# A fused attention and gated-MLP kernel: a PSUM bank, a normalisation, and the order of the first batch

## The chip, the cores and the metric

The kernel runs on one core of a Trainium2 chip. The metric is the device time of one execution in microseconds; the lower the better. The core has five engines that run their own instruction streams in order and meet through semaphores: PE (matrix multiply), DVE (vector), ACT (scalar and activation functions), POOL (GpSimd) and SP, which here only issues DMAs. PE writes to PSUM, which is used here as eight banks.

## The reference

Grouped-query attention over 8 batches, then a gated MLP whose gate mixes along the sequence. Cut to what matters:

```python
# q (8, 16, 384, 64); k, v (8, 4, 384, 64); each k, v head serves 4 q heads
attn = softmax(q @ k.T / sqrt(64))          # rows sum to 1
x = (attn @ v), heads side by side          # (8, 384, 1024)
h = maximum(x @ w_in, 0)                    # w_in (1024, 1024)
u, v = h[..., :512], h[..., 512:]
v_n = (v - mean(v)) / sqrt(var(v) + 1e-6)   # over the 512 columns
v_s = einsum('ts,bsd->btd', w_spatial, v_n) + b_spatial[None, :, None]
out = (u * v_s) @ w_out                     # w_out (512, 1024), out float32
```

## The kernel before

**Two streams on PE.** Attention is written as steps. A batch has NU = 18 of them: six groups m (three query tiles qt times two head blocks j), each with three key tiles t. `scores(n)` (L224) makes one step's scores: two matmuls `sc` of a 64-row contraction (L233), one for each half of the rows, and one exponential on ACT that writes `aT` (L240). Two score tiles exist (pool ps_sc, bufs=2). `weigh(b, m, hh)` (L242) multiplies a group's three `aT` tiles with v: 12 matmuls `av` (L247) into the one bank of pool ps_av; then DVE takes the reciprocal `r` of the row sums (L257) and writes the normalised `x` (L259). `x_transposes` (L271) turns x into `xt` with PE (four transposes `xps`, a DVE copy, L276); later batches use DMA transposes (`x_turn`, L278) instead. `q_transposes` (L195) and `k_transposes` (L185) do the same for q and k of batches 0 and 1, their copies on DVE (L205, L193).

The MLP is a generator, `stream()` (L467), which hands out one matmul at a time and says how many columns it took. `v_tile(b, st)` (L288) makes one tile of 128 tokens of v: eight matmuls `pv` (L294), one for each 128 of the contraction; the first four read the blocks of xt that group m = 2 st gives, the last four those of m = 2 st + 1. After the eighth, DVE takes `vr` (maximum with 0, L304), `stats` and the aggregate `mv` (L306, L307). `normal(b)` (L311) makes v_n: ACT computes `rstd` by Ln and Exp (L314, L315), DVE `nmr` = -mean * rstd (L316), then POOL computes vr * rstd + nmr for the tiles `vn` (L327; in the last batch, tile 1 on DVE and tile 2 on ACT, L324). `u_tile` and `u_block` make u, `gate` the spatial product `psp` (L378) and the gating, `project` the output.

**The order.** It is written out by hand, and no scheduler changes it. The loop at L637 takes the steps n one after another; in each: DMAs and casts due at this step (`todo`), scores, the two halves of `weigh` (group m's first half at step 18b + 3m + 3, its second one step later), the `turns` due at this step (transposes, idle matmuls), and then `run_fill(cols)` (L631), which draws matmuls from the stream until the credit of columns is used up. HV = 8 x 512 columns is the work of one v tile. Up to step 17, scores are issued one step ahead, one a step; from step 18 two at each even step. In the first batch the fill gets a quarter of HV at steps 10 to 13 and two fifths at 16 to 20. Batch 0's x transposes of group m stand at step 3m + 6, for m = 5 at 20; its q transposes of (j, t) at 3(2t + j) - 3; k and q transposes of batch 1 at 14 to 16, 19 and later.

**Banks.** Pool ps_ck has three banks under one tag, "ck". Every transposed tile, pv, pu, psp and po takes one in turn, and gives it back when its last reader is done. The tile `warm` (L543) takes one for the idle matmuls of `keep_warm` (L545), which multiply the identity with itself and whose result nobody reads; as one tile serves all calls, its bank is held from the first call to the last, at step 15. The calls are of 27, 4 and 6 matmuls before the first scores, and then of 4 each at steps 0 to 9, 14 and 15.

**Loads.** w_in comes as four DMAs from POOL (L121): the v columns of contraction blocks 0 to 3, then of 4 to 7, then the u columns in the same two halves. POOL also casts k, q and v to fp16 ahead of each batch.

Of the kernel before, what the change touches and what calls it, by code (L numbers as in the profile page):

```python
# [9 lines left out]
FP32 = mybir.dt.float32  # L10
FP16 = mybir.dt.float16
AF = mybir.ActivationFunctionType
ALU = mybir.AluOpType
# [4 lines left out]
def kernel(  # L18
# [16 lines left out]
    nc = tc.nc  # L35
    P = 128
    B, HQ, S, D = q.shape
# [4 lines left out]
    NT = S // P  # L42
# [4 lines left out]
    scale = D ** -0.5  # L47
    VW = D + 2
    NU = 18
# [7 lines left out]
    small = ctx.enter_context(tc.tile_pool(name="small", bufs=4))  # L57
# [3 lines left out]
    ps_ck = ctx.enter_context(tc.tile_pool(name="ps_ck", bufs=3, space=PSUM))  # L61
# [29 lines left out]
    def load_q0(j, lo, hi, eng):  # L91
# [18 lines left out]
            name=nc.get_next_instruction_name(), act_func_set_id=set_id, ins=[], outs=[]  # L110
# [113 lines left out]
    def scores(n):  # L224
        b, r = divmod(n, NU)
        m, t = divmod(r, NT)
        qt, j = divmod(m, 2)
        if t == 0:
            aTs[b, m] = att.tile([P, NT, 2, 512], FP16, name=f"aT_{b}_{m}", tag="aT", bufs=3)
        sc = ps_sc.tile([P, 2, 512], FP32, name=f"sc_{b}_{m}_{t}", tag="sc")  # L230
        for hh in range(2):
            half = slice(hh * D, (hh + 1) * D)
            nc.tensor.matmul(  # L233
                sc[:, hh],
                kTs[b][half, j, t * P : (t + 1) * P],
                qTs[b, j][half, qt],
                start=True,
                stop=True,
            )
        nc.scalar.activation(aTs[b, m][:, t], sc, AF.Exp, scale=scale)  # L240

    def weigh(b, m, hh):  # L242
        qt, j = divmod(m, 2)
        av = ps_av.tile([P, G, D + 1], FP32, name=f"av_{b}_{m}_{hh}", tag="av")
        for i in range(G):
            for t in range(NT):
                nc.tensor.matmul(  # L247
                    av[:, i, :],
                    aTs[b, m][:, t, hh, i * P : (i + 1) * P],
                    v1[b % 2][:, 2 * j + hh, t, 0 : D + 1],  # L250
                    start=(t == 0),
                    stop=(t == NT - 1),
                )
        if m == 0 and hh == 0:
            x16s[b] = att.tile([P, NT, NB, P], FP16, name=f"x16_{b}", tag="x16")
        r = small.tile([P, G, 1], FP32, name=f"r_{b}_{m}_{hh}", tag="r")
        nc.vector.reciprocal(r, av[:, :, D : D + 1])  # L257
        blk = 4 * j + 2 * hh
        nc.vector.tensor_tensor(  # L259
            x16s[b][:, qt, blk : blk + 2].rearrange("p k (i d) -> p (k i) d", i=2),  # L260
            av[:, :, 0:D],
            r.to_broadcast([P, G, D]),
            ALU.mult,
        )
# [21 lines left out]
    mvs, v_rs, v_ns, uTs, gTs, osbs = {}, {}, {}, {}, {}, {}  # L286
# [22 lines left out]
        yield 512  # L309

    def normal(b):  # L311
        rstd = small.tile([P, NT], FP32, name=f"rstd_{b}", tag="rstd")
        nmr = small.tile([P, NT], FP32, name=f"nmr_{b}", tag="nmr")
        nc.scalar.activation(rstd, mvs[b][:, :, 1], AF.Ln, bias=eps_t)  # L314
        nc.scalar.activation(rstd, rstd, AF.Exp, scale=-0.5)  # L315
        nc.vector.scalar_tensor_tensor(  # L316
            nmr, mvs[b][:, :, 0], -1.0, rstd, op0=ALU.mult, op1=ALU.mult
        )
        v_ns[b] = []
        for st in range(NT):  # L320
            vn = moe.tile([P, DH], FP16, name=f"vn_{b}_{st}", tag="vn", bufs=6)
            a, c = rstd[:, st : st + 1], nmr[:, st : st + 1]
            if b == B - 1 and st == 2:
                nc.scalar.activation(vn, v_rs[b][st], AF.Identity, scale=a, bias=c)  # L324
            else:
                by = nc.vector if b == B - 1 and st == 1 else nc.gpsimd
                by.tensor_scalar(vn, v_rs[b][st], a, c, op0=ALU.mult, op1=ALU.add)  # L327
            v_ns[b].append(vn)

    def uT_tile(b):  # L330
# [4 lines left out]
    def u_tile(b, st):  # L335

        pu = ps_ck.tile([P, NM, P], FP32, name=f"pu_{b}_{st}", tag="ck")
        for m in range(NM):
            for kt in range(NB):
                if st == 1 and m == 1 and kt == 0:  # L340
                    normal(b)
                nc.tensor.matmul(  # L342
                    pu[:, m],
                    w_in16[:, kt, m * P : (m + 1) * P],
                    x_tile(b)[:, st, kt],
                    start=(kt == 0),
                    stop=(kt == NB - 1),
                )
                if m < NM - 1 or kt < NB - 1:
                    yield P  # L350
        nc.vector.tensor_scalar(
            uT_tile(b)[:, :, st * P : (st + 1) * P], pu, 0.0, None, op0=ALU.max
        )
        yield P

    def u_block(b, m):
        pu = ps_ck.tile([P, 512], FP32, name=f"pu_{b}_{m}", tag="ck")
        for kt in range(NB):
            nc.tensor.matmul(  # L359
                pu[:, 0:S].rearrange("p (t s) -> p t s", t=NT),  # L360
                w_in16[:, kt, m * P : (m + 1) * P],
                x_tile(b)[:, :, kt],
                start=(kt == 0),
                stop=(kt == NB - 1),
            )
            if m == 0 and kt == 3:
                normal(b)
            if kt < NB - 1:
                yield S
        nc.scalar.activation(uT_tile(b)[:, m, :], pu[:, 0:S], AF.Relu)  # L370
        yield S
# [123 lines left out]
    HV = NB * 512  # L495
# [41 lines left out]
    def turn_at(n, f, *args):  # L537

        turns.setdefault(n, []).append((f, args))

    by_dve, by_act = nc.vector.tensor_copy, nc.scalar.copy

    warm = ps_ck.tile([P, 512], FP32, name="warm", tag="ck")  # L543

    def keep_warm(n):  # L545
        for _ in range(n):
            nc.tensor.matmul(warm[:, 0:P], ident16, ident16, start=True, stop=True)  # L547

    keep_warm(27)
    cast_k(0, dve, (0,))  # L550
    cast_q(0, 0, dve, 0, 1, by_act)
    k_transposes(0, 0, by_dve)
    keep_warm(4)
    q_transposes(0, 0, 0, by_act, by_dve)
    keep_warm(6)
    scores(0)
    cast_k(0, pool, (1,))
# [18 lines left out]
    for j in range(2):  # L576
        for t in (1, 2):
            turn_at(3 * (2 * t + j) - 3, q_transposes, 0, j, t, by_dve)
    for n in (*range(10), 14, 15):
        turn_at(n, keep_warm, 4)  # L580
    at(9, cast_k, 1, pool)
    at(10, cast_q, 1, 0, pool)
# [46 lines left out]
    total = NU * B  # L629

    def run_fill(cols):  # L631
        nonlocal owed
        owed += cols
        while owed > 0:
            owed -= next(fill, 1e9)

    for n in range(total + 6):  # L637
        for f, args in todo.pop(n, []):
            f(*args)
        if n + 1 < NU:  # L640
            scores(n + 1)
        elif n >= NU and n % 2 == 0 and n < total:
            scores(n)
            scores(n + 1)
        for hh in range(2):
            b, r = divmod(n - 3 - hh, NU)
            if n >= 3 + hh and r % 3 == 0 and b < B:
                weigh(b, r // 3, hh)
        for f, args in turns.pop(n, []):
            f(*args)  # L650
        if n < NU + 3:

            run_fill(HV / 4 if 10 <= n < 14 else 2 * HV / 5 if 16 <= n else 0)
        elif n < 2 * NU + 4:
            run_fill((4 * HV + NM * NT * S + 6 * NM * 512) / (NU + 4 - 3))
        else:
            run_fill(COLS / NU)
# [31 lines left out]
```

## Time and profile before

| | us |
|---|---|
| median of 3 runs | 251.71 (251.39 to 252.03) |
| profiled execution | 251.51 |
| its span, first to last instruction | 249.7 |
| ACT busy | 169.1 |
| DVE busy | 139.9 |
| POOL busy | 97.4 |

The span is what the trace covers; the rest of the profiled execution's time lies around it. The timeline gives for each merged group of instructions its start, its length, engine, line, operation, tiles (out<-in), shapes and count, and in brackets the idle time of the engine before it with what ended it. A group's length on PE holds the drain of its last matmul, so consecutive PE groups overlap; the start of the next group tells when PE went on. PEld is PE's weight load, which runs beside its matmuls.

Landings of the first DMAs that the steps below need, by the trace: w_in's v columns at 13.50 and 16.86 us, its u columns at 25.42 and 27.86; k of batch 1 at 18.07, its q halves at 20.48 and 22.84, its v at 29.06.

### The profile page before, as it was taken

What the parts mean: (1) busy time and instruction counts of PE and PEld (TensorE: products, weight loads), DVE (VectorE), ACT (ScalarE), POOL (GpSimd) and SP (SyncE); (2) the same over time, 40 slices, a digit from 0 to 9 for tenths busy, and PEclk for the clock granted to TensorE, in tenths of its full rate; (3) what the DMA queues carried; (4) which work ended last, traced back from release to release, by engine and by line L of the source; (5) the groups of instructions that cost most, each with busy time, mean ns of one, the idle gap of its engine ahead of it and who ended that gap; (6) DMA issues with size and microseconds to landing.
All of it is one profiled execution on the core that took longest, in us unless ns stands there. A gap on an engine that the chain in (4) does not pass through costs nothing.

```text
span 249.7 us, 6038 instructions
## 1 busy us (share of the span) xinstructions
PE 240.9 (96%) x2438; PEld 126.2 (51%) x2438; DVE 139.9 (56%) x370; ACT 169.1 (68%) x217; POOL 97.4 (39%) x141
## 2 busy tenths in 40 slices
PE   7998998999999999999999999999999999999993
PEld 7564666634455445544455445544455444554551
DVE  2455777764546646375536746375536746375662
ACT  3896665777686677868686677868686687862231
POOL 2698836881034800393034800393034000350130
PEclk9999999999999999999999999999999999999999
DMA  7999998999379973996479973999474172024206
GB/s 180 269 285 252 301 281 238 289 233 265 104 145 326 173 276 66 236 274 178 168 145 333 169 273 71 206 302 175 171 151 90 24 273 45 0 46 168 84 26 230
DMA packets 73980, 46.93 MB, mean 188 GB/s; under 512 B 48112, under 2 KB 68912, under 8 KB 73952
## 3 DMA queue, kind: packets, MB, share of 16 engines
q1 hardware_dynamic: 68832, 37.63, 59.2%
q0 software_dynamic: 4080, 8.65, 13.9%
q8 instruction: 19, 0.31, 0.5%
q10 hardware_dynamic: 1040, 0.26, 0.5%
q14 instruction: 9, 0.07, 0.1%
HBM read 25.95 MB, written 12.58 MB: 154 GB/s over the span
## 4 chain that ended last, share of the span: by engine, by line
PE 91%; DVE 6%; ACT 1%; issue 1%; POOL 0%; POOLq 0%
PE av L247 17%; PE pv L294 16%; PE sc L233 15%; PE po L449 15%; PE pu L359 14%; PE psp L378 6%; PE warm L547 3%; DVE x L259 2%; DVE stats L306 1%; DVE vr L304 1%; PE pu L342 1%; PE qps L200 1%; ACT aT L240 1%; PE psp L402 1%; PE xps L275 1%
## 5 line engine op out<-in xcount | busy, mean ns | idle before, releaser
L240 ACT ACTIVATE aT<-sc 128x1024 f16<-128x1024 f32 x144 | 139.6, 1021 | 53.3 <-PE sc L233 53.1
L247 PEld LDWEIGHTS <-aT 128*128 128x128 f16 x1152 | 43.4, 97 | 32.9 <-DVE x L259 12.8
L327 POOL TENSOR_SCALAR vn<-vr,rstd,nmr 128x512 f16<-128x512 f32 x22 | 16.9, 778 | 100.0 <-DVE r L257 86.2
L247 PE MATMUL av<-v,aT 128*128 128x65 f16 x1152 | 52.4, 194 | 1.6 <-DVE x L259 1.2
L257 DVE RECIPROCAL r<-av 128x4 f32<-128x4 f32 x96 | 17.2, 179 | 58.3 <-PE av L247 57.7
L294 PE MATMUL pv<-w_in,xt 128*128 128x512 f16 x192 | 49.6, 379 | 0.0
L449 PE MATMUL po<-w_out,gT 128*128 128x512 f16 (+2 forms) x196 | 47.9, 375 | 0.0
L233 PE MATMUL sc<-qT,kT 64*128 64x512 f16 x288 | 45.4, 385 | 0.5 <-DVE qT L205 0.3
L259 DVE TENSOR_TENSOR x<-av,r 128x256 f16<-128x256 f32 x96 | 40.8, 425 | 3.4
L359 PE MATMUL pu<-xt,w_in 128*128 128x384 f16 x216 | 40.2, 326 | 0.0
L389 POOL TENSOR_TENSOR gT<-g,uT 128x384 f16<-128x384 f32 x28 | 24.7, 914 | 26.8 <-DVE g L388 26.8
L359 PEld LDWEIGHTS <-w_in 128*128 128x128 f16 x216 | 19.4, 98 | 14.2 <-issue 2.5
L170 POOL CAST q<-q 128x768 f16<-128x768 f32 (+1 forms) x36 | 24.9, 733 | 3.1 <-DMA q<-in_q_dram 3.1
L449 PEld LDWEIGHTS <-gT 128*128 128x128 f16 x196 | 16.9, 97 | 18.3 <-issue 2.9
L294 PEld LDWEIGHTS <-xt 128*128 128x128 f16 x192 | 16.1, 97 | 13.5 <-issue 0.6
L458 DVE COPY osb<-po 128x512 f32<-128x512 f32 (+1 forms) x25 | 16.7, 667 | 11.1 <-PE po L449 11.1
L233 PEld LDWEIGHTS <-kT 64*128 64x128 f16 x288 | 8.9, 94 | 26.4 <-issue 24.0
L304 DVE TENSOR_SCALAR vr<-pv 128x512 f32<-128x512 f32 x24 | 16.5, 688 | 10.2 <-PE pv L294 10.0
L458 ACT COPY osb<-po 128x512 f32<-128x512 f32 (+1 forms) x24 | 14.0, 584 | 10.6 <-PE po L449 10.5
L306 DVE BATCH_NORM_STATS2 stats<-vr 128x6 f32<-128x512 f32 x24 | 16.7, 695 | 0.8
L378 PE MATMUL psp<-wsT,vn 128*128 128x384 f16 x84 | 17.0, 327 | 0.0
L388 DVE TENSOR_TENSOR g<-psp,bias_b 128x384 f32<-128x384 f32 x28 | 14.4, 552 | 2.7 <-PE psp L378 2.7
(59 smaller groups left out, 136.2 us busy)
## 6 DMA issues: line engine op xcount, KB each, us to landing
out_dram<-osb SPq DMA_DIRECT2D x21, 512.0 KB, 2.9
q<-in_q_dram SPq DMA_DIRECT2D x10, 768.0 KB, 7.1
q<-in_q_dram POOLq DMA_DIRECT2D x4, 768.0 KB, 10.4
v<-in_v_dram SPq DMA_DIRECT2D x6, 384.0 KB, 8.7
w_in<-in_moe_w_in_dram POOLq DMA_DIRECT2D x4, 512.0 KB, 9.8
k<-in_k_dram SPq DMA_DIRECT2D x5, 384.0 KB, 4.1
out_dram<-osb SPq DMA_DIRECT2D x5, 256.0 KB, 2.0
q<-in_q_dram SPq DMA_DIRECT2D x2, 512.0 KB, 7.2
```

What stands on the lines that cost most here:

```text
L170: f(q16s[b, j][:, lo:hi, :, hh, :], src[:, hh, lo:hi])
L233: nc.tensor.matmul(sc[:, hh], kTs[b][half, j, t * P : (t + 1) * P], qTs[b, j][half, qt], start=True, stop=True,)
L240: nc.scalar.activation(aTs[b, m][:, t], sc, AF.Exp, scale=scale)
L247: nc.tensor.matmul(av[:, i, :], aTs[b, m][:, t, hh, i * P : (i + 1) * P], v1[b % 2][:, 2 * j + hh, t, 0 : D + 1], start=(t == 0), stop=(t ...
L259: nc.vector.tensor_tensor(x16s[b][:, qt, blk : blk + 2].rearrange("p k (i d) -> p (k i) d", i=2), av[:, :, 0:D], r.to_broadcast([P, G, D]) ...
L294: nc.tensor.matmul(pv, x_tile(b)[:, st, kt], w_in16[:, kt, DH:DFF], start=(kt == 0), stop=(kt == NB - 1),)
L306: nc.vector.bn_stats(stats, vr)
L359: nc.tensor.matmul(pu[:, 0:S].rearrange("p (t s) -> p t s", t=NT), w_in16[:, kt, m * P : (m + 1) * P], x_tile(b)[:, :, kt], start=(kt == 0 ...
L378: nc.tensor.matmul(psp[:, 0:S], v_ns[b][st][:, m * P : (m + 1) * P], wsT16[:, st, :], start=(st == 0), stop=(st == NT - 1),)
L389: nc.gpsimd.tensor_tensor(gTs[b][:, m, :], g, uTs[b][:, m, :], ALU.mult)
L449: nc.tensor.matmul(po[:, 0 : hi - lo], gTs[b][:, m, tt * P : (tt + 1) * P], w_out16[:, m, lo:hi], start=(m == 0), stop=(m == NM - 1),)
L458: (nc.scalar.copy if half and not i else nc.vector.tensor_copy)(osb[:, lo:hi], po[:, 0 : hi - lo])
```

## The change

The bank of the idle matmuls is taken anew in each call, instead of once for all, and the calls at steps 6 to 9, 14 and 15 are gone. The normalisation is (vr + minus) * rstd with minus = -mean, so DVE's small instruction reads only `mv`; for the tile that ACT makes in the last batch DVE also computes `ac` = minus * rstd for this tile. Scores 1 to 12 are issued one step ahead as before, score 13 at step 13, and then two at each even step from 14. The fill of the first batch begins at step 6 with one pv a step (an eighth of HV) up to step 9, two at 10 and 11, none at 12, a sixth of HV at 13 to 15, a quarter at 16 and 17 and a third at 18 to 20.

```diff
     def normal(b):
         rstd = small.tile([P, NT], FP32, name=f"rstd_{b}", tag="rstd")
-        nmr = small.tile([P, NT], FP32, name=f"nmr_{b}", tag="nmr")
+        minus = small.tile([P, NT], FP32, name=f"minus_{b}", tag="minus")
         nc.scalar.activation(rstd, mvs[b][:, :, 1], AF.Ln, bias=eps_t)
         nc.scalar.activation(rstd, rstd, AF.Exp, scale=-0.5)
-        nc.vector.scalar_tensor_tensor(
-            nmr, mvs[b][:, :, 0], -1.0, rstd, op0=ALU.mult, op1=ALU.mult
-        )
+        nc.vector.tensor_scalar(minus, mvs[b][:, :, 0], -1.0, None, op0=ALU.mult)
+        if b == B - 1:
+            ac = small.tile([P, 1], FP32, name="ac", tag="ac")
+            nc.vector.tensor_tensor(ac, minus[:, 2:3], rstd[:, 2:3], ALU.mult)
         v_ns[b] = []
         for st in range(NT):
             vn = moe.tile([P, DH], FP16, name=f"vn_{b}_{st}", tag="vn", bufs=6)
-            a, c = rstd[:, st : st + 1], nmr[:, st : st + 1]
+            a, c = minus[:, st : st + 1], rstd[:, st : st + 1]
             if b == B - 1 and st == 2:
-                nc.scalar.activation(vn, v_rs[b][st], AF.Identity, scale=a, bias=c)
+                nc.scalar.activation(vn, v_rs[b][st], AF.Identity, scale=c, bias=ac)
             else:
                 by = nc.vector if b == B - 1 and st == 1 else nc.gpsimd
-                by.tensor_scalar(vn, v_rs[b][st], a, c, op0=ALU.mult, op1=ALU.add)
+                by.tensor_scalar(vn, v_rs[b][st], a, c, op0=ALU.add, op1=ALU.mult)
...
-    warm = ps_ck.tile([P, 512], FP32, name="warm", tag="ck")
-
     def keep_warm(n):
+        warm = ps_ck.tile([P, 512], FP32, name="warm", tag="ck")
         for _ in range(n):
             nc.tensor.matmul(warm[:, 0:P], ident16, ident16, start=True, stop=True)
...
-    for n in (*range(10), 14, 15):
+    for n in range(6):
         turn_at(n, keep_warm, 4)
...
-        if n + 1 < NU:
+        if n < 12:
             scores(n + 1)
-        elif n >= NU and n % 2 == 0 and n < total:
+        elif n == 13:
+            scores(n)
+        elif n % 2 == 0 and n > 13 and n < total:
             scores(n)
             scores(n + 1)
...
-            run_fill(HV / 4 if 10 <= n < 14 else 2 * HV / 5 if 16 <= n else 0)
+            at_n = {6: 8, 7: 8, 8: 8, 9: 8, 10: 4, 11: 4, 13: 6, 14: 6, 15: 6, 16: 4, 17: 4}
+            run_fill(HV / at_n[n] if n in at_n else HV / 3 if n >= NU else 0)
```

## The prediction

> **What bounds the kernel now.** I read the page first: busy shares, clock and the chain.
>
> ```profile
> span 249.7 us, 6038 instructions
> PE 240.9 (96%) x2438; PEld 126.2 (51%) x2438; DVE 139.9 (56%) x370; ACT 169.1 (68%) x217; POOL 97.4 (39%) x141
> PEclk9999999999999999999999999999999999999999
> PE 91%; DVE 6%; ACT 1%; issue 1%; POOL 0%; POOLq 0%
> ```
>
> PE holds 91% of the chain, so an edit is worth what it takes out of, or puts into, PE's in-order sequence. The busy column can't price this, because matmul rows overlap; I use the distance from one start to the next in the timeline. The first batch, steps 6 to 12:
>
> ```profile
> 13.71 0.39 PE L200 MATMUL qps<-ident,q 128*128 128x128 f16 x4
> 13.93 0.39 PE L547 MATMUL warm<-ident 128*128 128x128 f16 x4
> 14.13 0.42 DVE L259 TENSOR_TENSOR x<-av,r 128x256 f16<-128x256 f32 x1
> 14.15 0.39 PE L275 MATMUL xps<-ident,x 128*128 128x128 f16 x4
> 14.47 0.41 DVE L205 COPY qT<-qps 128x512 f16<-128x512 f16 x1
> 14.47 0.39 PE L233 MATMUL sc<-qT,kT 64*128 64x512 f16 x2
> 14.80 0.41 DVE L276 COPY xt<-xps 128x512 f16<-128x512 f16 x1
> ...
> 20.42 0.39 PE L200 MATMUL qps<-ident,q 128*128 128x128 f16 x4
> 20.62 0.18 DVE L257 RECIPROCAL r<-av 128x4 f32<-128x4 f32 x1 [1.45 <-PE av L247]
> 20.84 0.42 DVE L259 TENSOR_TENSOR x<-av,r 128x256 f16<-128x256 f32 x1
> 21.18 0.41 DVE L205 COPY qT<-qps 128x512 f16<-128x512 f16 x1
> 21.65 0.38 PE L275 MATMUL xps<-ident,x 128*128 128x128 f16 x4 [0.84 <-DVE qT L205]
> ```
>
> See two things. The x transposes of 14.15 reach xt only at 15.21, because DVE takes r, x, the qT copy and the xt copy in that order; nobody reads xt yet. And at 20.42 four q transposes (0.22) are followed by x transposes 1.23 later: a 1.0 us wait for a bank, since pv and the idle matmuls hold two of the three "ck" banks. Then the list of waits (who waited for whom: us in total, times, the longest), and the timeline where batch 0 is normalised:
>
> ```profile
> DVE nmr L316 <- ACT rstd L315: 9.9, 8, 1.5
> ```
>
> ```profile
> 38.76 0.89 PE L342 MATMUL pu<-xt,w_in 128*128 128x128 f16 x13
> 39.46 0.16 DVE L316 SCALAR_TENSOR_TENSOR nmr<-mv,rstd 128x3 f32<-128x3 f32 x1 [0.60 <-ACT rstd L315]
> 39.54 0.18 DVE L257 RECIPROCAL r<-av 128x4 f32<-128x4 f32 x1
> 39.75 0.42 DVE L259 TENSOR_TENSOR x<-av,r 128x256 f16<-128x256 f32 x1
> 40.23 0.55 PE L247 MATMUL av<-v,aT 128*128 128x65 f16 x12 [0.58 <-DVE x L259]
> ```
>
> DVE's nmr waits for ACT's rstd, r and x stand behind it, and PE waits for x.
>
> **Unit prices**, as distances between starts in the timeline: four transposes or idle matmuls 0.22 (17.09 to 17.31); an av group 0.38; one pv 0.216 (seven from 27.07); one score pair of matmuls 0.32, two pairs together 0.54 (28.67 to 29.21), and 0.09 for each change of form ahead of them. An exponential begins 0.44 after its scores, lasts 1.02, its reader starts 0.05 later. DVE begins r 0.20 after an av group ends, x 0.21 later for 0.42, copies then 0.33 apart; vr, stats and aggr delay it 1.55. A reader on PE starts 0.06 after a DVE copy.
>
> **Part 1, idle matmuls.** Calls at steps 6 to 9, 14 and 15 go: 6 x 0.22 = -1.34. PE has hardly an unfilled gap there, so it is real. In steps 0 to 5 each call takes its own bank in turn; by the trace, the DVE copies of those banks end before (qT copy 11.52 to 11.93, idle matmuls of step 5 at 12.68), so no cost.
>
> **Part 2, scores by two from 13.** Singles 14 to 17 become two pairs: each saves 0.32 x 2 + 0.09 - 0.54 = 0.19, together -0.38. The lead of the exponentials shrinks, below.
>
> **Part 3, v earlier; a walk through PE's order.** What starts at 13.01 (score 7) is as before. Step 6: without the idle matmuls the x transposes end at 14.15, and the first pv is next on PE. It reads xt, whose copy still stands on DVE behind r, x and qT, from 14.80 to 15.21: the pv starts at 15.27, **wait 1.11**. The first half of w_in's v columns has landed at 13.50, the second at 16.86 (queue view), both in time. Steps 7 to 11 hold four pv in place of idle matmuls (0.216 for 0.22) and two each at 10 and 11; score 8 is at 15.58 instead of 14.47, a wait of 0.10 for xt at step 10, end of step 11 at 20.77 with v's first tile done. Step 12: the first av of group m=3 runs to 21.15, but DVE has the finished tile's vr, stats and aggr ahead of its r (vr at 20.98, r at 22.53, x to 23.16). PE's transposes and step 13's score end at 22.01. The second av has only the bank that x is still reading: it starts at 23.21, **wait 1.20**, and the next pv waits 0.30 for xt, which is copied behind that x. Step 14: scores 14 and 15 at 24.41; exponential 14 is done at 25.87, but PE reaches step 15's av at 25.34: **wait 0.58**. Step 15 has k, q and x transposes, one bank each, while pv of tile 1, open since step 13, holds one of the three: the x transposes, due at 26.69, take k's, whose copy stands behind r and x on DVE (27.05 to 27.40): **wait 0.77**, the old 1.0 of step 12 in another place. Step 18 waits 0.13 for exponential 17. Tile 1 ends with step 17, so its statistics (30.23 on) hold x to 32.41: **wait 0.45** at step 19. The last half of w_in's u columns landed at 27.86, u begins after 31: covered. Score 20 is at 33.77, and the first av of batch 1 waits for its exponential until 35.28 (0.18). Before, that av started at 33.90 with one pv more behind it: the front is 35.28 + 0.22 - 33.90 = **+1.6** late. Cross-check: new waits 4.8, old ones -1.4 (1.0 here, 0.3 at 32.5, small ones), parts 1 and 2 -1.7: +1.7.
>
> No DMA is issued from a moved step by PE or DVE; POOL's loads hang on POOL's own order, which stays. From step 21 on the orders are the same: credits for the fill are equal at step 20 (3 tiles' worth in both).
>
> **Part 4, mean on POOL.** minus needs no rstd. Batch 0: aggr ends 38.86, minus takes at most nmr's 0.16, r, x then end near 39.57, av 39.63 instead of 40.23: -0.60. Batches 1 to 6 each have one score pair with 0.62 instead of 0.54 to the next av, where nmr has waited 1.45 (in batch 2: nmr 99.51, scores 99.66, av 100.28): -0.08 x 6 = -0.49. Batch 7: POOL's vn starts at 236.03 after nmr, and the first spatial matmul waits 0.1 for it: -0.1. Sum **-1.2**. Not in the trace: POOL's add-then-multiply. Bounds: vn's row (778 ns) and the dearer two-tensor row of POOL (914), so 0 to 0.14 each, and down by as much if it is cheaper; I take 0, the same instruction and operands. Three of them end at 102.05, the first reader is at 104.43; uncovered only in batch 7, 0.14. minus and ac: between the 0.06 of a one-column memset and nmr's 0.16.
>
> **Sum.** +1.6 - 1.2 = +0.4 on the profiled 251.51 (span 249.7 and 1.8 around it), which is 0.2 under the median of the runs: forecast 251.71 + 0.4 = **252.1**, its own range 251.4 to 252.7 (the cross-check's 0.1, POOL's 0.14, the bank variant's 0.8 below, and half of part 4's 0.5 in batches 1 to 6 above).
>
> **Clock.** From 7.40 to 9.40 PE stands idle for 0.33 and 0.46 of 2 us (7.82 to 8.15, 8.93 to 9.40), and the next idle matmuls still run 0.22 for four; so PE's new waits should not slow it.
>
> **Rivals.**
> *Slower: DVE keeps what nmr gave up.* The 1.2 of part 4 comes only if x was late for nmr alone. For it: the score pair of 53.33 is followed by av only at 54.37, 1.04 instead of 0.54, for an x that stands behind stats with no nmr near; in batch 0 stats and aggr end just before. It decides where r would start without nmr: if later than 39.5, nothing returns. Against: nmr's wait is in each of the 8 batches, and DVE idles in it. Price: 251.71 + 1.6 = 253.3.
> *Slower: the clock falls* in steps 12 to 16, where a third of the time is waiting. PE does some 3 us of work there, and while it was cold 27 idle matmuls took from 1.62 to 4.48, 106 ns each for 55 later, so +3 on the forecast: 255. Against: the clock row, and the stretch above. The Trainium skill, page "TensorE: Matmul & The Clock Gate", section "A second HAM failure mode: psum-queue depth-cycling", speaks for it: frequent small idle gaps of PE, from cycling through PSUM banks, can make its clock fall and rise again. No row here shows that yet.
> *Faster: the early v is absorbed.* If PE doesn't pay at step 6 and step 13 (1.11 + 1.20 + 0.30), the front is -1.0 and the sum -2.2: 249.5. For it: PE's and ACT's idle time in the early steps; against: DVE's order, plain in the rows above.
> *The bank does nothing*: without the bank back, step 15 and step 6 would wait more; with it, step 15 still waits. That is in the forecast; if step 15 finds a bank, -0.8: 251.3.
>
> **Chances.** A measurement of this kernel can tell about 0.3% (0.75 us) from no change. Forecast, with the bank variant: 0.50 (0.42 within that bound, 0.06 slower, 0.02 faster). DVE keeps it: 0.27 (0.25 slower, 0.02 within). Clock: 0.06, slower. Absorbed: 0.17 (0.14 faster, 0.03 within). So faster 0.16, same 0.47, slower 0.37. The range reaches over the second case with 0.3 to spare and leaves out the clock and most of the absorbed case: 250.8 to 253.6.
>
> **What would show it.** Right: a PE wait of about 1.1 before the first pv near 15.3; step 13's second av near 23.2 behind vr and stats; an x-transpose wait at step 15; no DVE wait for rstd but in batch 7; score pairs all 0.54; the first batch-1 av near 35.3. Wrong: that av before 34.3 or after 36.3, four idle-size matmuls above 0.25 after step 6, or the waits of L247 at x unchanged from batch 1 on.

## The result and the profile after

The changed kernel takes 252.38 us (median of 20 runs, 251.84 to 253.35), the kernel before 251.48 us in runs taken beside them (251.11 to 252.10). The ratio is 1.0032, with a 95% interval of 1.0023 to 1.0042: 0.8 to 0.9 us slower, just over the 0.75 us that was called no change, and inside the predicted range. The profiled execution has a span of 250.8 us, 1.1 more than before's; each trace is one execution, and this pair differs by a little more than the medians do.

The page of the kernel after, same lines as were shown of before:

```profile
span 250.8 us, 5989 instructions
PE 239.5 (95%) x2414; PEld 125.1 (50%) x2414; DVE 140.9 (56%) x371; ACT 169.0 (67%) x217; POOL 97.4 (39%) x141
PEclk9999999999999999999999999999999999999998
PE 87%; DVE 6%; DMA 3%; POOL 1%; ACT 1%; issue 1%; POOLq 0%
```

PE is busy 1.4 us less and the span is longer, so PE waits more. The clock row shows no fall in the first batch (it says little of the first 4.5 us, where it stands at 9 too while 27 idle matmuls take 106 ns each). A name is new in the chain: DMA, 3%.

The timeline of the kernel after, at steps 6 and 12 to 15 (start, length, engine, line, operation, tiles, and in brackets the engine's idle time before it with what ended it):

```profile
13.71 0.39 PE L200 MATMUL qps<-ident,q 128*128 128x128 f16 x4
13.93 0.39 PE L275 MATMUL xps<-ident,x 128*128 128x128 f16 x4
14.12 0.42 DVE L259 TENSOR_TENSOR x<-av,r 128x256 f16<-128x256 f32 x1
14.46 0.41 DVE L205 COPY qT<-qps 128x512 f16<-128x512 f16 x1
14.79 0.41 DVE L276 COPY xt<-xps 128x512 f16<-128x512 f16 x1
15.26 0.39 PE L294 MATMUL pv<-w_in,xt 128*128 128x512 f16 x1 [0.95 <-DVE xt L276]
...
21.02 0.69 DVE L304 TENSOR_SCALAR vr<-pv 128x512 f32<-128x512 f32 x1 [0.76 <-PE pv L294]
21.75 0.69 DVE L306 BATCH_NORM_STATS2 stats<-vr 128x6 f32<-128x512 f32 x1
22.48 0.18 DVE L307 BATCH_NORM_AGGREGATE mv<-stats 128x2 f32<-128x6 f32 x1
22.58 0.15 DVE L257 RECIPROCAL r<-av 128x4 f32<-128x4 f32 x1
22.76 0.42 DVE L259 TENSOR_TENSOR x<-av,r 128x256 f16<-128x256 f32 x1
23.24 0.55 PE L247 MATMUL av<-v,aT 128*128 128x65 f16 x12 [1.11 <-DVE x L259]
...
25.95 0.48 PE L247 MATMUL av<-v,aT 128*128 128x65 f16 x10 [0.35 <-ACT aT L240]
...
27.43 0.38 PE L275 MATMUL xps<-ident,x 128*128 128x128 f16 x4 [0.60 <-DVE kT L193]
```

The four large waits of the walk are there, at their places: the first pv for the xt copy (13.93 + 0.22 to 15.26, 1.11), the second av of group 3 for an x that stands behind vr, stats and aggr (1.2 by starts), step 15's av for exponential 14, and the x transposes for the bank of k's. The bracket is smaller than the wait by starts, since the drain of the matmul before counts as busy.

The list of waits and the timeline of the kernel after where batch 0 is normalised:

```profile
POOL vn L330 <- ACT rstd L317: 99.8, 8, 17.7
```

```profile
40.16 0.18 DVE L307 BATCH_NORM_AGGREGATE mv<-stats 128x2 f32<-128x6 f32 x1
40.25 0.89 PE L345 MATMUL pu<-xt,w_in 128*128 128x128 f16 x13
40.38 0.17 DVE L318 TENSOR_SCALAR minus<-mv 128x3 f32<-128x3 f32 x1
40.46 0.18 DVE L257 RECIPROCAL r<-av 128x4 f32<-128x4 f32 x1
40.67 0.42 DVE L259 TENSOR_TENSOR x<-av,r 128x256 f16<-128x256 f32 x1
41.15 0.55 PE L247 MATMUL av<-v,aT 128*128 128x65 f16 x12
```

The wait for rstd is POOL's now. DVE goes from aggr to minus, r and x at once; the av is 0.90 behind the start of pu instead of 1.47.

What the prediction did not have, in the timeline of the kernel after at step 36, the first scores of batch 2:

```profile
55.66 1.67 PE L452 MATMUL po<-w_out,gT 128*128 128x512 f16 x7
57.91 0.61 PE L233 MATMUL sc<-qT,kT 64*128 64x512 f16 x4 [0.57 <-DMA qT<-q]
```

The same place before:

```profile
54.75 1.67 PE L449 MATMUL po<-w_out,gT 128*128 128x512 f16 x7
56.35 0.60 PE L233 MATMUL sc<-qT,kT 64*128 64x512 f16 x4
```

Seven po and the change of form take 1.61 (54.75 to 56.35 before); after, the scores come after 2.25, so PE waits 0.64 for the DMA that transposes q of batch 2.

Starts of the same instruction in the two traces make the ledger. Second av of batch 1: 35.56 and 37.04, +1.48. Second av of its group 1, past the normalisation: 40.23 and 41.15, +0.92. First av of its group 5, past step 36: 56.89 and 58.45, +1.56. From there each batch takes 0.08 back where nmr stood: 72.22 and 73.70 (+1.48), 100.28 and 101.67 (+1.39), at last 212.50 and 213.56 (+1.06).

### The profile page after: what moved, and what is told of

It is laid out like the page before. It is cut to its first block, busy times and chain, and to the rows that moved or that the text cites. A ratio compares the mean times of both kernels' runs of the same rounds, so it can differ in the third digit from the quotient of the medians.

```text
span 250.8 us, 5989 instructions
## 1 busy us (share of the span) xinstructions
PE 239.5 (95%) x2414; PEld 125.1 (50%) x2414; DVE 140.9 (56%) x371; ACT 169.0 (67%) x217; POOL 97.4 (39%) x141
## 3 DMA queue, kind: packets, MB, share of 16 engines
HBM read 25.95 MB, written 12.58 MB: 154 GB/s over the span
## 4 chain that ended last, share of the span: by engine, by line
PE 87%; DVE 6%; DMA 3%; POOL 1%; ACT 1%; issue 1%; POOLq 0%
PE av L247 16%; PE pv L294 16%; PE sc L233 15%; PE po L452 14%; PE pu L362 14%; PE psp L381 5%; DMA qT<-q 3%; PE warm L549 2%; PE pu L345 2%; DVE x L259 2%; ACT aT L240 1%; POOL gT L392 1%; DVE stats L306 1%; DVE vr L304 1%; PE psp L405 1%
## 5 line engine op out<-in xcount | busy, mean ns | idle before, releaser
L330 POOL TENSOR_SCALAR vn<-vr,minus,rstd 128x512 f16<-128x512 f32 x22 | 16.9, 779 | 99.8 <-ACT rstd L317 99.8
```

## The experiments

All times are beside runs of before on the same chip; kernels from different rounds ran on different chips, so the ratios are the safer comparison between them. In the traces the first av starts anywhere from 9.62 to 10.37 us, which is not explained here; differences of starts are read with that taken off.

| kernel | median, us | ratio to before (95%) |
|---|---|---|
| e1: normalisation alone | 250.75 | 0.9960 (0.9944 to 0.9976) |
| e2: all but the normalisation | 253.50 | 1.0067 (1.0041 to 1.0094) |
| e3: after, old fill | 250.44 | 0.9958 (0.9939 to 0.9977) |
| e4: after, loads of batch 3 moved | 251.91 | 1.0016 (0.9993 to 1.0039) |
| e5: old fill, loads moved | 248.84 | 0.9896 (0.9884 to 0.9907) |
| e6: before, loads moved | 251.46 | 1.0004 (0.9995 to 1.0014) |
| e7: e4 with the first pv at step 7 | 251.04 | 0.9984 (0.9975 to 0.9993) |
| e8: e5 with single scores | 248.97 | 0.9903 (0.9891 to 0.9915) |
| e9: e4, tile 0 ends at step 13 | 249.76 | 0.9929 (0.9916 to 0.9942) |
| e10: e9 with the first pv at step 7 | 249.02 | 0.9905 (0.9892 to 0.9917) |
| e11: e5 with the idle matmuls back | 249.52 | 0.9920 (0.9906 to 0.9934) |

The theory: the front costs 1.5 us by four nameable waits, the normalisation gives 1.1 back, and a DMA at step 36 takes 0.6. The rivals are those of the prediction, and that the DMA wait is an accident of the one trace.

**The parts by themselves.** e1 is before with the new `normal(b)`; e2 is after with the old one.

```diff
 e1, to the kernel before:
-        nc.vector.scalar_tensor_tensor(nmr, mvs[b][:, :, 0], -1.0, rstd, op0=ALU.mult, op1=ALU.mult)
+        nc.vector.tensor_scalar(minus, mvs[b][:, :, 0], -1.0, None, op0=ALU.mult)
...
 e2, to the kernel after: the same lines the other way
```

> The kernel before, with part 4 alone (mean subtracted on POOL). Theory: DVE no longer waits for rstd, so av of batch 0 comes 0.55 to 0.6 us earlier, batches 1 to 6 gain 0.08 each and the last 0.1: -0.9 to -1.2 us against before (ratio 0.995 to 0.9965); a little of it may go to the DMA-transposed qT of batch 2, which landed 0.5 us before its first reader in the trace of before. Rival (DVE keeps what nmr gave up): statistics hold x anyway, 0 to -0.2 us, and the score pairs before the late av stay at 0.62.

> The kernel after, with before's normalisation put back: parts 1 to 3 alone. Theory: the first av of batch 1 stays near 35.0 (+1.1 to +1.5 on before), PE's waits in batch 0 are those of after, and at step 36 it waits another 0 to 0.7 us for qT of batch 2: +1.5 to +2.1 us on before (ratio 1.006 to 1.0085). Rival (front and normalisation interact: the 0.57 of batch 0 is only there because the new front shifts DVE): +0.8 to +1.1, as after.

e1: -0.8 us by the medians, a little under the expected -0.9 to -1.2, with a ratio inside the expected range. DVE does not keep what nmr gave up: that rival is out. Its trace has the 0.57 of batch 0 and the 0.08 in each of batches 1 to 6, and loses 0.7 at step 36 and another 0.39 among the first scores of batch 6, again waiting for a qT. This execution was the slowest of its 12 runs (251.37), so a typical run probably loses less. The timeline of e1 at step 36:

```profile
53.98 1.67 PE L452 MATMUL po<-w_out,gT 128*128 128x512 f16 x7
56.29 0.61 PE L233 MATMUL sc<-qT,kT 64*128 64x512 f16 x4 [0.64 <-DMA qT<-q]
```

PE came earlier, the transpose did not. e2 has the front without the normalisation's gain, +1.7 us by the ratio; its trace has 1.49 of front and a wait of 0.37 at step 36. The two halves add up within their intervals (1.0067 and 0.9960 make 1.0027 together, after has 1.0032), so no sign is seen that the gain of the normalisation hangs on the new front.

**The early fill.** e3 gives the kernel after the fill of before.

```diff
-            at_n = {6: 8, 7: 8, 8: 8, 9: 8, 10: 4, 11: 4, 13: 6, 14: 6, 15: 6, 16: 4, 17: 4}
-            run_fill(HV / at_n[n] if n in at_n else HV / 3 if n >= NU else 0)
+            run_fill(HV / 4 if 10 <= n < 14 else 2 * HV / 5 if 16 <= n else 0)
```

> The kernel after with before's fill of the first batch (a quarter of HV at steps 10 to 13, two fifths from 16 to 20): parts 1, 2 and 4 alone. Theory, PE order: no pv waits at step 6, no x behind the statistics at step 13, so the first av of batch 1 starts near 32.2 instead of 35.04 and by PE alone the kernel takes 3 us less than before. Theory, DMA: qT of batch 2 can't land much before 55, since its DMAs stand behind the loads, so PE waits 1 to 2.5 us at step 36 and -0.8 to -1.6 us on before remains (ratio 0.9935 to 0.997). Rival to the first (early v is not what costs the front): first av of batch 1 at 34 or later, time as after or above before.

Both halves of the theory hold. In e3's trace the second av of batch 1's group 1 starts at 37.52, 2.7 us ahead of before (0.4 of it from the start of that run), and the whole kernel is only 1.1 us faster. The timeline of e3 at step 36 has the rest:

```profile
52.03 1.67 PE L452 MATMUL po<-w_out,gT 128*128 128x512 f16 x7
55.41 0.61 PE L233 MATMUL sc<-qT,kT 64*128 64x512 f16 x4 [1.70 <-DMA qT<-q]
```

3.38 instead of 1.61: a wait of 1.77. So the loss of the front is the early fill's, and a faster front is worth little while qT lands where it does. e3 also shows what the bank is worth when no early pv takes it: at step 12 the x transposes follow q's after 0.22 (19.02 to 19.25), where before had 1.23, and at step 15 too. No run changes the bank alone.

**The transposes behind the loads.** SP's queue of the kernel after, around the loads of batch 3 (start, length of the issue, line, operation), and two of the same issues before:

```profile
42.41 2.04 SPq L279 DMA_TRANSPOSE xt<-x  x1
44.58 0.50 SPq L79 DMA_DIRECT2D k<-in_k_dram  x1
45.18 1.06 SPq L85 DMA_DIRECT2D q<-in_q_dram  x2
46.35 2.16 SPq L82 DMA_DIRECT2D v<-in_v_dram  x1
48.61 2.76 SPq L208 DMA_TRANSPOSE kT<-k  x1
51.47 5.94 SPq L215 DMA_TRANSPOSE qT<-q  x2
```

```profile
41.49 1.34 SPq L279 DMA_TRANSPOSE xt<-x  x1
...
47.08 2.77 SPq L208 DMA_TRANSPOSE kT<-k  x1
```

e4 issues those loads two steps later, behind the transposes of k and q; e5 does it with the old fill, e6 with the kernel before.

```diff
             if b > 2:
-                at(w0 - NU + 11, load_k, b)
+                at(w0 - NU + (13 if b == 3 else 11), load_k, b)
...
```

> The kernel after with the loads of batch 3 issued at step 31 behind batch 2's DMA transposes of k and q instead of at step 29 ahead of them. Theory (PE's wait of 0.64 us at step 36 is for a transpose that queues behind 2.3 MB of loads): that wait goes, -0.4 to -0.7 us on after, level with before (ratio 0.999 to 1.0015). Rival (the wait only shifts: the transposes share DMA engines with the loads in any order, or the loads come late for batch 3): as after, or slower with a new wait near 66 to 85 us.

> Old fill (parts 1, 2 and 4) with the loads of batch 3 behind batch 2's transposes. Theory: the old fill brought PE 2.3 us ahead of before by batch 1 (2.71 with the start of that run 0.40 early) and lost 1.8 of it at step 36 on qT; with the loads moved the wait is under 0.2, and the later gains (0.08 a batch, 0.1) come on top: -2.5 to -3.0 us on before (ratio 0.988 to 0.990). Rival (PE's wait at step 36 is DMA bandwidth, not order): as with the old fill alone, 0.996.

> The kernel before with the loads of batch 3 moved alone. Theory: in the trace of before qT landed 0.5 us ahead of its reader, so there is no wait to take away: 0 (ratio 0.9985 to 1.001). Rival (the moved loads help or hurt by themselves, whatever the front): -0.5 us or more, or slower.

SP's queue of e4:

```profile
42.01 1.86 SPq L279 DMA_TRANSPOSE xt<-x  x1
44.00 1.21 SPq L208 DMA_TRANSPOSE kT<-k  x1
45.35 3.31 SPq L215 DMA_TRANSPOSE qT<-q  x2
48.76 0.86 SPq L79 DMA_DIRECT2D k<-in_k_dram  x1
```

kT lands 2.7 us after its issue there (44.00 to 46.73), against 8.0 in the kernel after (48.61 to 56.59), and the scores of step 36 follow po after 1.61 without a wait. By the clock e4 alone is not clear (1.0016, with an interval that reaches 1.0039); e5 against e3 is: 0.9896 against 0.9958, 1.6 us for the same edit. In e6 the edit is worth nothing, as expected: before had no such wait, its qT landed at 55.83 and was read at 56.35. The wait is no accident of one trace: it is 0.64, 0.71, 0.37 and 1.77 in after, e1, e2 and e3, and absent in all eight kernels with the loads moved.

So, with the same bytes to move, the order on SP's queue decides whether PE waits at step 36. The Trainium skill, page "DMA: Bandwidth & Descriptors", section "Queues, rings and completion order", says that each DMA engine takes descriptors of one issuing queue in ring order; these traces agree: in the kernel after v, kT and qT land at 54.37, 56.59 and 57.78, in the order of their issue. Later batches of the same kernel already have the transpose of k ahead of the next loads, and there it lands 2.8 to 4.5 us after its issue. Whether the loads would hold the transposes from another queue too, no run shows.

Order is not all. In e3 the x transpose at the head of SP's queue is issued at 38.77 and lands at 44.81; before's is issued at 41.49 and lands at 45.04. From 38.8 to 41.5 the queue of POOL's loads, those of batch 2 last, takes 95% of the time of the 16 DMA engines in e3's trace. So an earlier front finds them taken, which fits e3's qT landing at 55.27, only 0.56 ahead of before's. In e5 the moved loads also give 0.33 us back: a pv at 59.79 waits for an xt whose transpose now stands behind them, the shift that the rival of e4 had named.

**Which of the front's waits cost.** e7 moves only the first pv, from step 6 to 7. e9 keeps it at step 6, but ends tile 0 (and so its statistics) at step 13 and draws tile 1 as a whole at 16 and 17. e10 does both. All have the loads moved.

```diff
-            at_n = {6: 8, 7: 8, 8: 8, 9: 8, 10: 4, 11: 4, 13: 6, 14: 6, 15: 6, 16: 4, 17: 4}
+            at_n = {7: 8, 8: 8, 9: 4, 10: 4, 11: 4, 13: 6, 14: 6, 15: 6, 16: 4, 17: 4}           # e7
+            at_n = {6: 8, 7: 8, 8: 8, 9: 8, 10: 8, 11: 8, 13: 4, 16: 2, 17: 2}                   # e9
+            at_n = {7: 8, 8: 8, 9: 8, 10: 8, 11: 8, 12: 8, 13: 4, 16: 2, 17: 2}                  # e10
```

> The kernel after with the moved loads, and the first pv at step 7 instead of 6 (one pv at 7 and 8, two at 9 to 11). Theory (1.1 us of the front is the first pv behind DVE's r, x and qT copy): the first pv then waits 0.3 instead of 1.11, while the second av of step 13 still waits 1.1 to 1.2 behind the statistics: -0.7 to -0.9 us on the kernel after with moved loads (ratio to before 0.998 to 0.9995). Rival (the wait at step 6 was absorbed later, in ACT's lead): no change from 1.0016.

> The kernel after with the moved loads, first pv still at step 6, one pv a step to step 11, two at 13, so that tile 0 and its statistics end at step 13; tile 1 as a whole at 16 and 17. Theory: 1.1 us at step 6 stays; the second av of group 3 no longer waits for an x behind the statistics (1.2 and 0.3 us), and as no pv is open at step 15 the x transposes find a bank (0.8); some of it comes back as a wait for exponential 14: -1.9 to -2.2 us on the kernel after with moved loads (1.0016), ratio to before 0.9925 to 0.9945. Rival (those waits are interchangeable, each gone one shows up elsewhere): above 0.998.

> As that, with the first pv at step 7 and one pv a step to 12: early v without the wait at step 6. Theory: the first pv waits 0.3 instead of 1.1, another -0.8 us: level with the old fill with moved loads (0.9896), ratio 0.988 to 0.991. So early v by itself costs nothing and gains nothing, and its place does. Rival (early v fills PE's idle time in ACT's stretch): below 0.988.

e7 against e4: -0.9 us by the medians, -0.8 by the ratios. The timeline of e7 at step 7:

```profile
14.14 0.55 PE L247 MATMUL av<-v,aT 128*128 128x65 f16 x12
14.81 0.39 PE L294 MATMUL pv<-w_in,xt 128*128 128x512 f16 x1
```

0.67 from av to the first pv instead of 0.38: a wait of 0.29 where after has 1.11. e9 against e4: -2.2 us. The timeline of e9 at steps 12 to 15:

```profile
20.23 0.53 PE L247 MATMUL av<-v,aT 128*128 128x65 f16 x12
...
21.14 0.39 PE L233 MATMUL sc<-qT,kT 64*128 64x512 f16 x2
21.49 0.55 PE L247 MATMUL av<-v,aT 128*128 128x65 f16 x12
...
23.92 0.49 PE L247 MATMUL av<-v,aT 128*128 128x65 f16 x10 [0.55 <-ACT aT L240]
...
24.63 0.39 PE L275 MATMUL xps<-ident,x 128*128 128x128 f16 x4
```

The second av follows the score at once, and step 15's x transposes follow q's at once; the wait for exponential 14 stays, and grows from 0.52 in after to 0.71. So the waits are not interchangeable: of 2.2 us of waits removed, 2.0 came off the front. e10 is level with e5 by the clock (0.9905 and 0.9896). The traces are not level: from the second av of batch 0, at 11.44 in both, to the second av of group 1 of batch 1, e10 takes 0.36 us longer (38.05 against 37.69), and e5 loses the 0.33 at 59.79 afterwards. So the place of the early v decides most of its cost; that it can be had for nothing is not shown.

**Scores by two, and the idle matmuls.** e8 is e5 with the score lines of before; e11 is e5 with the idle matmuls' calls of before, each with its own bank.

```diff
 e8:
-        if n < 12:
-            scores(n + 1)
-        elif n == 13:
-            scores(n)
-        elif n % 2 == 0 and n > 13 and n < total:
+        if n + 1 < NU:
+            scores(n + 1)
+        elif n >= NU and n % 2 == 0 and n < total:
 e11:
-    for n in range(6):
+    for n in (*range(10), 14, 15):
         turn_at(n, keep_warm, 4)
```

> As the old fill with moved loads, but scores one a step up to 17 as before: parts 1 and 4 alone. Theory: two pairs save 0.38 us of PE and lose ACT's lead, one wait of 0.7 before the first av of step 15, so that singles are within 0.3 us of pairs, either way (ratio to before 0.987 to 0.991). Rival (part 2 is worth its 0.38 in full): 0.4 us slower than with pairs. Its trace should show no wait for an exponential at step 15.

> The old fill with moved loads, with the idle matmuls of steps 6 to 9, 14 and 15 put back, each call with its own bank. Theory: PE has a wait for exponential 8 there and less for 14, which hide part of the 1.34 us: +0.6 to +0.9 us on the kernel without them (ratio to before 0.992 to 0.9935). Rival (they are worth their 1.34 in full): 0.995. Rival (clock: without them PE's clock falls): they would make it faster than 0.9896; with them and without, four transposes take 0.22 us.

e8 is within 0.2 us of e5, not told apart. By the traces e5 waits 0.68 us for exponential 14, where e8 has no such wait but waits 0.46 for a bank at the x transposes of step 15; that takes 0.22 off the pairs' 0.38. e11 is 0.7 us slower than e5 (0.9920 against 0.9896), not 1.34: in part the idle matmuls only fill time in which PE would wait for ACT (0.44 at 15.55 and 0.68 at 22.92 in e5, none and 0.46 in e11). They do nothing for the clock: four transposes take 0.22 us with them and without.

The best of these, e5, e8 and e10, are 2.4 to 2.6 us faster than before and 3.4 to 3.5 faster than after.

## Why the prediction was right, and where not

The mechanism and the direction were right; one term of the sum was missing, and it is larger than the whole forecast of +0.4. That 252.38 still lies in the range is in part luck: the range was opened for the bank, for POOL's arithmetic and for the rivals, and none of these came. Against the ledger of the traces:

| term | predicted | measured |
|---|---|---|
| front, to batch 1 | +1.6 | +1.48 |
| normalisation, batch 0 | -0.60 | -0.56 |
| batches 1 to 6 | -0.49 | -0.50 |
| batch 7 | -0.1 | 0 |
| qT of batch 2 at step 36 | 0 | +0.64 |
| rest, to the end | 0 | +0.06 |
| sum, profiled execution's span | +0.4 | +1.12 |

**The front.** The walk through PE's order was confirmed wait by wait: first pv predicted at 15.27 and found at 15.26, the second av of group 3 at 23.21 and 23.24, step 15's av held to 25.92 and 25.95, its x transposes to 27.46 and 27.43, the first av of batch 1 at 35.28 and 35.04 (with its wait for the exponential ahead of its third matmul, at 35.22). e7 and e9 show that the first two are real costs and not absorbed, against the faster rival; the bank, given back, only moved its wait from step 12 to 15 under the new fill, as the walk had it, and e9, where no pv is open at step 15, loses it.

**The normalisation** was right in batches 0 to 6, and e1 shows it alone; POOL's add-then-multiply costs nothing (779 ns a tile against 778). Not all score pairs are 0.54 now: the one of 1.04 at 53.33, which the rival had cited, is still there (54.24 to 55.28), as nmr never stood near it. In batch 7 the prediction put a wait of 0.1 down to POOL's vn. It is still there: 0.268 from the last u matmul to the first spatial one against 0.271 before, though vn ends at 237.89, 0.3 ahead. The traces point to ACT: the first psp comes three tiles after the first u tile, whose bank it takes, and ACT's uT of this tile, which stands behind ACT's own vn, ends at 237.11 before and 238.16 after, 0.05 ahead of the psp in both. Before, POOL's vn ended beside it, at 237.05; so two waits ended together, and the change took away one. ACT's vn still waits for DVE, now for ac. No run tests this by itself.

**The step that failed** is "From step 21 on the orders are the same", with "No DMA is issued from a moved step" ahead of it, by which no wait was expected there: the term was put at 0 and is 0.64 in the trace (0.4 to 0.5 by the clock of after and e4, which is not clear of noise). The sentence holds for PE. But SP's queue begins with the x transpose of step 26, which waits for PE's x, and the loads of batch 3 and then the transposes of k and q for batch 2 stand behind it. In the trace of before qT landed 0.52 us ahead of its first reader, a margin that the DMA view shows and the prediction did not look up for steps after 21. The front pushed PE by 0.92 at that point; the landing moved by 1.95 (55.83 to 57.78), as the x transpose's issue took 2.04 instead of 1.34 and kT landed 8.0 instead of 7.5 us after its issue. That the transposes wait behind these loads is shown (e4, e5); why these two rows grew is not settled. e1, with PE earlier, has the wait as well (its x transpose's issue took 2.40), so it isn't a matter of delay alone.

**The clock rival** is out. Between 20.8 and 28.0 us PE waits 1.19, 0.27, 0.52 and 0.77, more than a third of the time, and four transposes at 28.88 still take 0.22; the windows view has the granted clock at 1.00 there. The fall that the Trainium skill, page "TensorE: Matmul & The Clock Gate", section "A second HAM failure mode: psum-queue depth-cycling", describes, and that was cited for this rival, does not show in these gaps of up to 1.2 us.

## What to carry to other kernels

When work is moved earlier on an in-order engine, walk what it reads back through the producer's queue: the producer's other work, in its written order, is the price, and it can exceed the idle time that the move was to fill. A tile's last instruction drags its eviction and statistics into the evicting engine's queue at that point; put it where no short-lived reader stands behind. And before trusting that later stages only shift, read the margin of each transfer that lands just ahead of its reader: a gain upstream can vanish there, and a loss can grow.

## What the runs showed of the hardware that was not expected

The same DMA transpose of k landed 7.5 to 8.1 us after its issue with 2.3 MB of loads ahead of it in SP's queue (before, after, e1 to e3). With the loads behind it, it took 2.7 to 2.9 us in e4, e6, e7 and e9, and 3.9 to 5.2 in e5, e8, e10 and e11, where it was issued 2.4 us or more before the last of POOL's loads landed, against at most 1.3 in the four others. The two score matmuls of a pair, with a 64-row contraction, start 3 to 4 ns apart, and each change between them and 128-row matmuls adds 0.09 to 0.10 us to the distance between starts, on the way in and on the way out; two pairs in a row therefore cost 0.54 where two single ones cost 0.64 and one more change. The value of the idle matmuls removed was about half their length (0.7 of 1.34 us, e11 against e5), since PE took part of the time back as a wait for ACT.
